# Dealing the products of the first gated step out among the last attention items

## The chip, the cores and the metric

The kernel runs on one NeuronCore of a Trainium2 chip. The metric is the device time of one execution in microseconds, as the median of several runs. In the rows below, PE is TensorE's matmuls and PEld its weight loads, DVE is VectorE, ACT is ScalarE, POOL is GpSimd and SP is SyncE, which issues most of the DMAs.

## What is computed

Three layers run one after the other.

```python
attn_out = _attn_ref(**attn_kwargs)          # 2 batches, 8 heads, 768 positions, head size 64
x = attn_out.transpose(0, 2, 1, 3).reshape(B * S, H * D)      # 1536 x 512
x = _moe_ref(x=x, **moe_kwargs)              # the gated layer
return _moe2_ref(x=x, **moe2_kwargs)         # eight experts, one for each token

def _moe_ref(x, w_gate, w_val, w_out, rms_g):
    rms = np.sqrt(np.mean(x * x, axis=-1, keepdims=True) + 1e-06)
    xn = x / rms * rms_g
    g = xn @ w_gate
    silu = g * (1.0 / (1.0 + np.exp(-g)))
    val = xn @ w_val
    return (silu * val @ w_out)
```

The attention adds a linear bias to the scores, keeps only local and a few global keys, and normalises with a softmax.

## The kernel before, in words

**Attention.** There are 24 items, numbered 0 to 23: eight pairs of heads times three groups of 256 queries. The loop in `attention` has 28 steps t = 0 to 27 and is a software pipeline five deep. In step t the item a = t gets its scores (`qk`, L243), its bias and row minimum (`ttr`, L254, DVE) and its exponentials (`exp`, L265, ACT). Item b = t - 1 is normalised (`zadd`, `zrec` and four times `norm`, L282). Item c = t - 2 is transposed on PE (`trans`, L289, two halves r = 0 and 1, up to three 128 x 128 transposes each) and copied out of PSUM, half 0 by DVE (`evac`, L298), half 1 by ACT (L300). Item d = t - 3 is multiplied with V (`pv`, L324). Item e = t - 4 is taken over by `out`, which calls `Rms.take` (L430 and L431 on ACT, L432 on DVE, for some items an addition L418 on POOL). In the steps up to 23 all four normalisations of an item run on GpSimd. In step 24, where item 23 is normalised, all four run on DVE.

**Order.** The order is written out by hand (`tc.manual_schedule()`): each engine executes its instructions in the order in which the program calls them, and waits on semaphores for its operands.

**Gated layer.** A step (i, c, a, b) computes columns 128 i to 128 i + 127 of `g` and of `val` for the tokens a to b of chunk c. Each of the two is a PSUM sum of 12 products (`gemm1`, L549): four slices of the model dimension times three combinations of high and low parts, in the order (wh, xh), (wh, xl), (wl, xh). The 24 products of a step thus use two weight units: the first 12 the unit (i, 0), the last 12 the unit (i, 1). `gate1` (L560 DVE, L562 ACT, L565 and L567 DVE) turns the two sums into the gated value. `step1` emits the products of one step and then the gate of the step before it.

**Weight units.** A unit arrives as raw float64 words and is unpacked by `unpack` in five pieces: an absolute value on ACT (L500), then L502, L507, L509 and L512 on DVE, then the high part by ACT (L514, `wh`) and the low part by POOL (L515, `wl`). The generator `unit` emits one piece after each attention step from t = 13. Unit 0 is emitted by t = 17, unit 1 by t = 22, unit 2 in t = 23 to 27. A step that finds too few units ready emits the missing pieces itself, just ahead of its products:

```python
    def gemm1s():
        z = done[0]
        done[0] += 1
        while len(ready) < 2 * (z // 2) + 2:
            next(unit)
        step1((z // 2, 1, 0, 256) if z % 2 else (z // 2, 0, 0, 512), silu=False)
```

**The four early steps.** Four gated steps need only tokens of the first batch and run beside the end of the attention. They are called A = (0, 0, 0, 512), B = (0, 1, 0, 256), C = (1, 0, 0, 512) and D = (1, 1, 0, 256) here. A and B use units 0 and 1, C and D units 2 and 3. Before the change A is emitted after step 25, B after step 26, C after step 27 and D after the square roots. In between, `rms[1].stats` (L455) sums the squares of the second batch on PE. `rms[1].root()` makes the inverse root in a chain of small DVE operations (L462 to L475) and ends with six diagonal tiles, three on DVE (L480) and three on ACT (L483). `spread` (L489 on PE, copied by ACT, L492) broadcasts it. After that comes the long list `order` of the other gated steps, which starts on PE with (0, 1, 256, 512).

Of the kernel before, what the change touches and what calls it, by code (L numbers as in the profile page):

```python
# [16 lines left out]
AX = mybir.AxisListType  # L17
PSUM = bass.MemoryType.PSUM
NEG = -1.0e9
FAST_LOCAL = 97  # L20
FAST_GLOBAL = 32
FAR = 1 << 20
# [21 lines left out]
def consts(s, ints):  # L44
# [25 lines left out]
    nc.vector.tensor_scalar(a[:, 0:1], s.nl, 1.0, None, ALU.is_ge)  # L70
    nc.vector.tensor_scalar(a[:, 1:2], s.nl, float(FAST_LOCAL), None, ALU.is_le)
    nc.vector.tensor_scalar(a[:, 2:3], s.ng, float(FAST_GLOBAL), None, ALU.is_le)
# [21 lines left out]
def bias_tiles(s):  # L94
# [12 lines left out]
    nc.vector.scalar_tensor_tensor(out=keep, in0=key, scalar=s.ng, in1=keep, op0=ALU.is_lt, op1=ALU.max)  # L107
    nc.vector.tensor_scalar(miss, keep, 1.0, -8.0 * NEG, ALU.subtract, ALU.mult)
    nc.vector.tensor_scalar(rel, rel, s.nl, None, ALU.min)
# [8 lines left out]
def general_attention(s):  # L118

    nc, tc = s.nc, s.tc  # L120
    with tc.tile_pool(name="ga", bufs=1) as p, tc.tile_pool(name="gap", bufs=1, space=PSUM) as ps:
# [3 lines left out]
        with tc.For_i(0, 8, 1) as pr:  # L125
            slope = p.tile([128, 2], F32, name="gslope")
            nc.vector.tensor_copy(slope, slopes[:, ds(pr, 1), :].rearrange("p a b -> p (a b)"))
            for hh in range(2):
# [17 lines left out]
                with tc.For_i(0, 6, 1) as i:  # L146
# [18 lines left out]
                    nc.vector.tensor_tensor(t, t, keep, ALU.mult)  # L165
                    nc.vector.tensor_scalar(keep, keep, 1.0, -NEG, ALU.subtract, ALU.mult)
                    nc.vector.tensor_tensor(t, t, keep, ALU.add)
# [24 lines left out]
def attention(s, rms):  # L192
# [6 lines left out]
    nc, ap = s.nc, s.apool  # L199
# [4 lines left out]
    def tick():  # L204
        next(s.small, None)
# [20 lines left out]
    def part(g, r, x):  # L226

        i = 2 * g + r
        if i == 0:
            return 0, s.kinds[x], 128 + 128 * x, 64 + 64 * x  # L230
        return 160 * (i - 1) + 32 + 64 * x, s.kinds[2 + x], 192 * x, 192

    def qk(it, t):
        pr, g = it

        sc = [s.ps_g.tile([128, 2, 256], F32, name=f"sc{x}", tag=f"ps{x}", bufs=2) for x in range(2)]
        for r in range(2):
            for h, x in ((0, 0), (1, 1), (0, 1), (1, 0)):
                k0, _, _, n = part(g, r, x)
                d = slice(64 * h, 64 * h + 64)  # L240
                o = slice(64 * (h ^ x), 64 * (h ^ x) + 64)
                i = 128 * (2 * g + r) + 64 * x
                nc.tensor.matmul(sc[x][o, r, 0:n], lhsT=qs[pr][d, i:i + 64],  # L243
                                 rhs=ks[pr][d, k0:k0 + n], start=True, stop=True)
        m = ap.tile([128, 4], F32, name="m", bufs=4)
        z = ap.tile([128, 4], F32, name="z", bufs=4)
        st[it] = (sc, es[t % 3], m, z)
# [20 lines left out]
    def zadd(it):  # L268
        z = st[it][3]
        nc.vector.tensor_scalar(z, z, 1e-9, None, ALU.add)  # L270

    def zrec(it):
        z = st[it][3]
        nc.vector.reciprocal(z, z)

    def norm(it, r, x, eng):
        pr, g = it
        sc, e, m, z = st[it]
        _, _, e0, n = part(g, r, x)
        j = 2 * r + x  # L280
        one = (1.0, ALU.mult) if eng is nc.gpsimd else (None,)
        eng.tensor_scalar(e[:, r, e0:e0 + n], e[:, r, e0:e0 + n], z[:, j:j + 1], one[0], ALU.mult, *one[1:])  # L282

    def trans(it, r):
        pr, g = it
        e = st[it][1]
        pt = s.ps_n.tile([128, 3, 128], F32, name="pt", tag="rb", bufs=2)
        for k in range(1 if g == r == 0 else 0, 3):
            nc.tensor.transpose(pt[:, k, :], e[:, r, 128 * k:128 * k + 128], s.ident)  # L289
        pts = ap.tile([128, 3, 128], F32, name="pts", bufs=4)  # L290
        outs[it, r] = (pt, pts)

    def evac(it, r, eng):
        pr, g = it
        pt, pts = outs[it, r]
        k = slice(1 if g == r == 0 else 0, 3)
        if eng is nc.vector:
            nc.vector.tensor_copy(pts[:, k], pt[:, k])  # L298
        else:
            nc.scalar.copy(pts[:, k], pt[:, k])  # L300

    def pv(it, r):
        pr, g = it
        pts = outs.pop((it, r))[1]

        if r == 0:
            po = s.bank([128, 512], "po")
            outs[it] = po[:, 0:256].rearrange("p (a b) -> p a b", a=2)
            s.spare = po[:, 256:512]
        po = outs[it]  # L310
        i = 2 * g + r
        lo, hi = halves[pr % 3]

        def terms(hh):
            a, b = slice(64 * hh, 64 * hh + 64), slice(64 - 64 * hh, 128 - 64 * hh)
            yield 0, 1, lo[:, hh, i], a
            if i:
                yield 0, 0, vs[pr][:, hh, 2 * i - 1], a
                yield 1, 1, hi[:, hh, i - 1], b
            yield 1, 2, vs[pr][:, hh, 2 * i], b  # L320

        for n, two in enumerate(zip(terms(0), terms(1))):
            for hh, (x, k, v, c) in enumerate(two):
                nc.tensor.matmul(po[64 * hh:64 * hh + 64, r, 64 * x:64 * x + 64], lhsT=v,  # L324
                                 rhs=pts[:, k, c], start=i == 0 or n % 2 == 0, stop=i == 0 or n % 2 == 1)

    def out(it):
        pr, g = it
        po = outs.pop(it)
        rms[pr // 4].take(pr % 4, g, po.rearrange("p a b -> p (a b)"))  # L330

    items = [(pr, g) for pr in range(8) for g in range(3)]
    n = len(items)
# [12 lines left out]
    for t in range(n + 4):  # L346
        a, b, c, d, e = (items[t - z] if 0 <= t - z < n else None for z in range(5))
        if a:
            qk(a, t)
        if c:  # L350
            trans(c, 0)
            trans(c, 1)
        if d:
            pv(d, 0)
            pv(d, 1)
        if b:
            zadd(b)
            tick()
            zrec(b)
            tick()  # L360
            if t < n:
                for r in range(2):
                    for x in range(2):
                        norm(b, r, x, nc.gpsimd)
            else:
                norm(b, 1, 1, nc.vector)
                norm(b, 0, 0, nc.vector)
            tick()
        if a:
            ttr(a, 0, 0)  # L370
            tick()
        if b and t >= n:
            norm(b, 0, 1, nc.vector)
            tick()
        if a:
            ttr(a, 0, 1)
            tick()
            ttr(a, 1, 0)
            tick()
        if b and t >= n:  # L380
            norm(b, 1, 0, nc.vector)
            tick()
        if a:
            ttr(a, 1, 1)
            tick()
        if c:
            evac(c, 0, nc.vector)
        if e:
            out(e)
        for half in range(2):  # L390
            if a:
                exp(a, half)
        if c:
            evac(c, 1, nc.scalar)
        if a:
            pr, g = a
            if g == 1 and pr + 2 < 8:
                load(pr + 2)
            if g == 2 and pr + 2 < 8:
                loadv(pr + 2)  # L400
        yield t
# [134 lines left out]
    return unpack(s, raw, s.wpool, hi, lo, eng)  # L536


def gemm1(s, i, c, a, b):

    nc = s.nc
    ps = []
    for z in range(2):
        p = s.ps_g.tile([128, b - a], F32, name=f"ps{z}", bufs=2)
        wh, wl = s.w[i, z]
        n = 0
        for k in range(4):
            for w, x in ((wh, s.xh), (wh, s.xl), (wl, s.xh)):
                nc.tensor.matmul(p, lhsT=w[:, k, :], rhs=x[c][:, k, a:b], start=n == 0, stop=n == 11)  # L549
                n += 1  # L550
        ps.append(p)
    s.gp[i, c, a, b] = ps


def gate1(s, i, c, a, b, silu=True):
# [407 lines left out]
def attn_moe_kernel(ctx, tc, qx, kx, vx, rel, ints, wgv, w_out, rms_g, w9, w9t, w1, w2, out):  # L963
    s = K()
    nc = s.nc = tc.nc
# [79 lines left out]
    done, behind = [0], []  # L1045

    def step1(x, *parts, silu=True):

        gemm1(s, *x)
        run(*parts, *[gate1(s, *behind.pop(0), silu) for _ in behind[:1]])  # L1050
        behind.append(x)

    def gemm1s():
# [3 lines left out]
            next(unit)  # L1057
        step1((z // 2, 1, 0, 256) if z % 2 else (z // 2, 0, 0, 512), silu=False)

    for t in att:  # L1060
        if t < 3:
            next(bias)
        if t == 4:
            load_unit(s, units[0])
            load_unit(s, units[1])
        if t >= 13:
            next(unit, None)
        if t == 16:
            with tc.If(flag == 0):
                rms[0].general(s.xg)  # L1070
        if t == 17:
            for g in range(3):
                rms[0].stats(g)
            s.small = rms[0].root()
        if 19 <= t < 22:
            run(s.small)
            rms[0].spread(t - 19)
        if t in (25, 26, 27):
            gemm1s()
        if t == 26:  # L1080
            ss = s.ps_n.tile([128, 133], F32, name="ss", tag="rb", bufs=2)
            rms[1].stats(0, ss)
            rms[1].stats(1)
        if t == 27:
            rms[1].stats(2)
# [161 lines left out]
    first = {}  # L1247
# [142 lines left out]
    with tc.For_i(1, more, 1) as j:  # L1390
# [3 lines left out]
        x = Expert(s, e, lgi, lsi, lgate)  # L1394
# [88 lines left out]
```

## Time and profile before

| what | value |
|---|---|
| runs | 539.6, 540.06, 542.44 us, median 540.06 us |
| profiled execution | 542.6 us, span 540.8 us from its first to its last instruction |
| busy in the span | PE 96%, DVE 74%, ACT 50%, POOL 27% |
| mean granted TensorE clock | 0.991 |

The profiled execution's own time is 1.8 us more than its span. Times in the rows are counted from the start of the span. An entry in square brackets is idle time of the engine just before the instruction, with what ended it. A row with "x4" merges four instructions in a run, and its second column reaches from the start of the first to the end of the last. Matmul durations overlap, so the distance between starts tells the rate.

### The profile page before, as it was taken

The numbers are of one execution on the slowest core, as the hardware profiler recorded it, in microseconds if no ns is written. First come the engines' busy times: TensorE is split into PE (matmuls) and PEld (weight loads), VectorE is DVE, ScalarE is ACT, GpSimd is POOL, SyncE is SP. The second block draws the span as 40 slices with busy tenths as digits, with TensorE's granted clock in tenths as the row PEclk, the third lists the DMA queues.
The fourth block names the chain that finished last, engine by engine and source line by source line (L and its number), as shares of the span: only waits on it lengthen the run. The fifth ranks groups of instructions, "written<-read, shape, count | busy, mean of one in ns | idle before, by whom it ended". The sixth has DMA issues, their size and how long they took to land. (4 is left out here: it accounts for less than half of the span.)

```text
span 540.8 us, 9801 instructions
## 1 busy us (share of the span) xinstructions
PE 516.5 (96%) x3408; PEld 420.9 (78%) x3408; DVE 402.2 (74%) x1016; ACT 272.4 (50%) x629; POOL 147.9 (27%) x198
## 2 busy tenths in 40 slices
PE   3999998999999999999999999999999999999994
PEld 2676776888888888888888887787888778888873
DVE  5888995578887688768875268667753699999961
ACT  2799995252332333333323343534532679888750
POOL 4577662101222212122212000000000603666001
PEclk9999997999999999999999999999999999999998
DMA  8798701203323323233305313123581799999300
GB/s 254 239 324 247 241 12 33 78 18 102 116 92 103 106 90 118 78 116 118 104 14 186 147 78 118 49 108 118 191 319 43 258 400 395 398 400 394 118 15 17
DMA packets 31001, 85.93 MB, mean 159 GB/s; under 512 B 3847, under 2 KB 4103, under 8 KB 30944
## 3 DMA queue, kind: packets, MB, share of 16 engines
q1 hardware_dynamic: 26400, 73.86, 39.4%
q0 software_dynamic: 2672, 8.22, 4.1%
q10 hardware_dynamic: 1872, 3.15, 1.7%
q8 instruction: 29, 0.48, 0.4%
q14 instruction: 28, 0.23, 0.1%
HBM read 77.52 MB, written 8.65 MB: 159 GB/s over the span
## 5 line engine op out<-in xcount | busy, mean ns | idle before, releaser
L549 PE MATMUL ps<-xh,wh 128*128 128x512 f32 (+1 forms) x304 | 115.7, 381 | 0.1
L549 PE MATMUL ps<-xh,wl 128*128 128x512 f32 (+1 forms) x304 | 115.2, 379 | 0.5 <-POOL wl L515 0.5
L549 PE MATMUL ps<-xl,wh 128*128 128x512 f32 (+1 forms) x304 | 115.1, 379 | 0.0
L875 DVE TENSOR_TENSOR ewl<-eraw,ewh 128x1024 fp32r<-128x1024 f32 x72 | 83.4, 1217 | 7.5 <-ACT ewh L866 7.3
L866 ACT CAST ewh<-eraw 128x1024 fp32r<-128x1024 f32 x72 | 71.4, 1055 | 6.8 <-DVE ewl L875 6.6
L549 PEld LDWEIGHTS ps<-xh,wl 128*128 128x128 f32 x304 | 57.3, 189 | 11.4 <-POOL wl L515 0.9
L549 PEld LDWEIGHTS ps<-xh,wh 128*128 128x128 f32 x304 | 57.4, 189 | 11.0 <-issue 0.2
L549 PEld LDWEIGHTS ps<-xl,wh 128*128 128x128 f32 x304 | 57.4, 189 | 10.7
L502 DVE SCALAR_TENSOR_TENSOR wraw<-f64t,wraw 128x512 f32<-128x512 f32 x36 | 43.9, 1219 | 28.8 <-ACT f64t L500 28.8
L625 PE MATMUL px<-woh,hh 128*128 128x512 f32 (+1 forms) x156 | 61.2, 392 | 0.0
L625 PE MATMUL px<-woh,hl 128*128 128x512 f32 (+1 forms) x156 | 58.4, 374 | 0.0
L515 POOL TENSOR_TENSOR wl<-f64t,wh 128x512 fp32r<-128x512 f32 x24 | 31.0, 1291 | 99.7 <-ACT wh L514 57.9
L625 PE MATMUL px<-wol,hh 128*128 128x512 f32 (+1 forms) x156 | 58.2, 373 | 0.0
L514 ACT CAST wh<-f64t 128x512 fp32r<-128x512 f32 x24 | 14.9, 621 | 71.5 <-DVE f64t L512 71.5
L265 ACT ACTIVATE es<-es,m 128x192 f32<-128x192 f32 (+1 forms) x96 | 41.3, 436 | 7.5 <-DVE m L254 7.5
L282 POOL TENSOR_SCALAR es<-es,z 128x192 f32<-128x192 f32 (+1 forms) x92 | 36.1, 411 | 25.3 <-PE pt L289 8.5
L579 DVE TENSOR_TENSOR hl<-h,hh 128x256 fp32r<-128x256 f32 x72 | 25.4, 421 | 17.8 <-ACT hh L578 17.8
L625 PEld LDWEIGHTS px<-woh,hh 128*128 128x128 f32 x156 | 29.4, 188 | 5.5 <-issue 0.9
L625 PEld LDWEIGHTS px<-woh,hl 128*128 128x128 f32 x156 | 29.3, 188 | 5.6
L625 PEld LDWEIGHTS px<-wol,hh 128*128 128x128 f32 x156 | 29.4, 189 | 4.1
L567 DVE TENSOR_TENSOR h<-sg,ps 128x512 f32<-128x512 f32 (+1 forms) x38 | 24.8, 651 | 10.4 <-PE ps L549 8.1
L243 PE MATMUL sc<-kd,qd 64*64 64x192 f32 (+2 forms) x384 | 24.1, 361 | 7.9 <-DVEq L1006 6.9
(208 smaller groups left out, 1003.7 us busy)
## 6 DMA issues: line engine op xcount, KB each, us to landing
eraw<-in_w_dram SPq DMA_DIRECT2D x64, 512.0 KB, 11.7
wraw<-in_wgv_dram SPq DMA_DIRECT2D x24, 512.0 KB, 3.9
wraw<-in_w_out_dram SPq DMA_DIRECT2D x12, 512.0 KB, 3.3
vp<-in_vx_dram SPq DMA_DIRECT2D x8, 704.0 KB, 7.5
eraw<-in_w_dram POOLq DMA_DIRECT2D x8, 512.0 KB, 15.4
kd<-in_kx_dram SPq DMA_DIRECT2D x7, 464.0 KB, 8.6
xm<-x SPq DMA_DIRECT2D x12, 256.0 KB, 2.6
out_dram<-x ACTq DMA_DIRECT2D x12, 256.0 KB, 2.9
```

The source lines that it names most:

```text
L243: nc.tensor.matmul(sc[x][o, r, 0:n], lhsT=qs[pr][d, i:i + 64], rhs=ks[pr][d, k0:k0 + n], start=True, stop=True)
L265: nc.scalar.activation(e[:, r, e0:e0 + n], e[:, r, e0:e0 + n], AF.Exp, bias=m[:, j:j + 1], scale=-1.0, accum_out=z[:, j:j + 1])
L282: eng.tensor_scalar(e[:, r, e0:e0 + n], e[:, r, e0:e0 + n], z[:, j:j + 1], one[0], ALU.mult, *one[1:])
L502: nc.vector.scalar_tensor_tensor(out=a.bitcast(F32), in0=t, scalar=F64_LEAST, in1=a.bitcast(F32), op0=ALU.is_ge, op1=ALU.mult)
L514: nc.scalar.copy(hi, t)
L515: eng.tensor_tensor(lo, t, f(hi), ALU.subtract)
L549: nc.tensor.matmul(p, lhsT=w[:, k, :], rhs=x[c][:, k, a:b], start=n == 0, stop=n == 11)
L567: nc.vector.tensor_tensor(u, sg, ps[1], ALU.mult)
L579: nc.vector.tensor_tensor(hl[:, i, :], src, f(hh[:, i, :]), ALU.subtract)
L625: nc.tensor.matmul(p, lhsT=h[:, k, :], rhs=w[k][:, c:c + N], start=n == 0, stop=n == 35)
L866: eng.copy(wh, raw)
L875: eng.tensor_tensor(wl, raw, f(wh), ALU.subtract)
```

## The change

The products of step A become a generator. `attention` calls `s.fill` in steps 23, 24, 25 and 26, right after `pv` and ahead of everything that the step emits for other engines, and takes 4, 5, 7 and the last 8 products from it (9 are asked for in step 26, the ninth call finds the generator at its end). Step A then counts as done. `gemm1s` is called only after step 27 instead of after steps 25, 26 and 27, so B is emitted there and C and D after the square roots. In step 24, item 23's half r = 0 is normalised on GpSimd (two operations) and half r = 1 on DVE (two operations), behind the copy of half 0 of item 22.

```diff
+FILL = {-1: 4, 0: 5, 1: 7, 2: 9}
@@ attention
+        s.fill(FILL.get(t - n, 0))
         if b:
             zadd(b)
             tick()
             zrec(b)
             tick()
-            if t < n:
-                for r in range(2):
-                    for x in range(2):
+            for r in range(2):
+                for x in range(2):
+                    if t < n or r == 0:
                         norm(b, r, x, nc.gpsimd)
-            else:
-                norm(b, 1, 1, nc.vector)
-                norm(b, 0, 0, nc.vector)
             tick()
         if a:
             ttr(a, 0, 0)
-            tick()
-        if b and t >= n:
-            norm(b, 0, 1, nc.vector)
             tick()
...
-        if b and t >= n:
-            norm(b, 1, 0, nc.vector)
-            tick()
         if a:
             ttr(a, 1, 1)
             tick()
         if c:
             evac(c, 0, nc.vector)
+        if b and t >= n:
+            norm(b, 1, 0, nc.vector)
+            norm(b, 1, 1, nc.vector)
         if e:
             out(e)
@@ gemm1 becomes a generator and a loop over it
-def gemm1(s, i, c, a, b):
+def products(s, i, c, a, b):
...
                 nc.tensor.matmul(p, lhsT=w[:, k, :], rhs=x[c][:, k, a:b], start=n == 0, stop=n == 11)
                 n += 1
+                yield
         ps.append(p)
     s.gp[i, c, a, b] = ps
+
+
+def gemm1(s, i, c, a, b):
+
+    for _ in products(s, i, c, a, b):
+        pass
@@ attn_moe_kernel
+    first = products(s, 0, 0, 0, 512)
+
+    def fill(n):
+        for _ in range(n):
+            if next(first, FAR) is FAR:
+                break
+        if n and (0, 0, 0, 512) in s.gp:
+            behind.append((0, 0, 0, 512))
+            done[0] += 1
+
+    s.fill = fill
...
-        if t in (25, 26, 27):
+        if t == 27:
             gemm1s()
```

## Rows read from the trace of the kernel before

**Rows 1.** The page's 40 slices: TensorE's granted clock, in tenths of full speed.

```profile
PEclk9999997999999999999999999999999999999998
```

**Rows 2.** PE's waits, 111 to 535 us: the costliest (total, times, longest).

```profile
PE rk L721 <- DVE oh L684: 0.7, 2, 0.4
```

**Rows 3.** Busy time by engine in stretches of 1 us, granted clock after POOL.

```profile
83.00:84.00 1.00, 0.78 (x11) 0.64 (x12) 0.96 (x2) 1.00 (x4) 0.97 (x2) 0.93 0.04 16
...
90.00:91.00 1.00, 1.00 (x4) 0.76 (x4) 0.94 (x2) 0.98 (x2) 0.00 (x0) 0.66 0.00 0
```

**Rows 4.** The timeline of PE from 68 to 115 us.

```profile
82.14 0.84 PE L289 MATMUL pt<-ident,es 128*128 128x128 f32 x3 [1.05 <-POOL es L282]
...
83.71 0.39 PE L324 MATMUL po<-pts,vlo 128*64 128x64 f32 x4
...
85.79 1.54 PE L289 MATMUL pt<-ident,es 128*128 128x128 f32 x6 [0.62 <-DVE pts L298]
87.26 0.48 PE L324 MATMUL po<-pts,vlo 128*64 128x64 f32 x4
...
95.56 0.34 PE L324 MATMUL po<-pts,vlo 128*64 128x64 f32 x4
...
96.64 0.39 PE L549 MATMUL ps<-xh,wh 128*128 128x256 f32 x1
...
99.62 1.84 PE L455 MATMUL ss<-ones,sq 128*128 128x1 f32 x16
101.32 0.48 PE L549 MATMUL ps<-xh,wh 128*128 128x512 f32 x1
...
104.36 0.39 PE L549 MATMUL ps<-xl,wh 128*128 128x512 f32 x1
105.22 0.50 PE L549 MATMUL ps<-xh,wl 128*128 128x512 f32 x1 [0.47 <-POOL wl L515]
...
107.65 0.95 PE L455 MATMUL ss<-ones,sq 128*128 128x1 f32 x8
108.75 0.36 PE L549 MATMUL ps<-xh,wh 128*128 128x256 f32 x1
...
111.70 1.06 PE L489 MATMUL rb<-rd,ones 128*128 128x128 f32 x8
113.39 0.71 PE L489 MATMUL rb<-rd,ones 128*128 128x128 f32 x4 [0.64 <-ACT rs L492]
113.86 0.36 PE L549 MATMUL ps<-xh,wh 128*128 128x256 f32 x1
```

**Rows 5.** The normalisations of L282 from 80 to 87 us: ns min/median/max.

```profile
L282 POOL TENSOR_SCALAR es<-es,z x4: 427/428/430, 81.7 to 82.9; 128x192 f32<-128x192 f32 x4
L282 DVE TENSOR_SCALAR es<-es,z x4: 306/550/929, 83.2 to 84.5; 128x192 f32<-128x192 f32 x4
```

**Rows 6.** The timeline of POOL from 66 to 115 us.

```profile
83.24 0.73 POOL L418 TENSOR_TENSOR sq<-sq 128x256 f32<-128x256 f32 x1
```

**Rows 7.** The timeline of DVE from 70 to 115 us.

```profile
86.05 0.68 DVE L502 SCALAR_TENSOR_TENSOR wraw<-f64t,wraw 128x512 f32<-128x512 f32 x1
...
99.88 1.29 DVE L502 SCALAR_TENSOR_TENSOR wraw<-f64t,wraw 128x512 f32<-128x512 f32 x1 [1.26 <-ACT f64t L500]
...
108.73 0.16 DVE L462 TENSOR_SCALAR rv<-ss 128x6 f32<-128x6 f32 x1 [2.76 <-PEq L1086]
```

**Rows 8.** The timeline of ACT from 72 to 112 us.

```profile
99.18 0.67 ACT L500 ACTIVATE f64t<-wraw 128x512 f32<-128x512 f32 x1
...
103.19 0.62 ACT L514 CAST wh<-f64t 128x512 fp32r<-128x512 f32 x1 [3.34 <-DVE f64t L512]
...
111.14 0.99 ACT L483 ACTIVATE rd<-ident,r 128x128 f32<-128x128 f32 x3 [7.01 <-DVE r L475]
```

**Rows 9.** Busy time by engine in stretches of 2 us at the end.

```profile
532.00:534.00 2.00, 1.37 (x6) 0.76 (x5) 0.59 (x1) 0.00 (x0) 0.00 (x0) 1.00 0.00 0
...
536.00:538.00 2.00, 0.00 (x0) 0.00 (x0) 0.00 (x0) 0.00 (x0) 0.00 (x0) 0.96 0.07 21
```

## The prediction

> **What bounds the kernel now.** I began with the page's 40 slices. Apart from the last slice, with the end of the run, only the seventh, around 81 to 95 us, has a granted TensorE clock clearly under full speed [rows 1]. That is where the attention ends and the gated layer begins, and the change sits there. Next I read PE's waits behind it: from 111 us to the end of the experts the costliest one adds up to 0.7 us [rows 2]. So PE sets the end, and a microsecond that PE gains or loses before about 114 us arrives at the end undiminished. The question is then only when PE starts the first step of the list `order`. Before, that is at 113.86 us [rows 4].
>
> The timeline of PE up to there shows what it loses. It waits 1.05 us for item 22's normalisations at 82.14, 0.62 us for DVE at 85.79, 0.47 us for unit 3's low part at 105.22 and 0.64 us at 113.39 [rows 4]. And the clock: the mean of 0.93 in 83 to 84 us puts its fall from 2.4 to 1.2 GHz near 83.86 us, the 0.66 in 90 to 91 us puts its rise near 90.68 us [rows 3]. That is 6.8 us at half speed. With the 0.62 us of waiting taken off, about 6.2 us of work could have taken 3.1 us. So idle time and clock together are worth 5.9 us, and the change reaches for nearly all of it.
>
> **The change, part by part.** *The tail of the attention.* Ahead of the wait at 82.14, four products are now queued. Fourteen products of this width start between 101.32 and 104.36, 0.23 us apart [rows 4], so four take 0.92 us and lie almost whole in the idle 1.05 us. They cost nothing; without that idle time they would cost their 0.92 us. What PE waited for at 82.14 (POOL) and up to 83.71 is untouched, so 83.71 stays [rows 4]. From there I add up PE's work at full clock until step C can start:
>
> - three `pv`: 1.08 us each (95.56 to 96.64), for item 21, a first group with six groups of matmuls in place of eight, 0.81: together 2.97 us [rows 4]
> - six transposes: 1.47 us at half clock (85.79 to 87.26), so 0.74 us [rows 4]
> - the remaining 20 products of A: 20 x 0.234 = 4.68 us
> - sums of squares: 1.70 us (99.62 to 101.32) and 1.10 us (107.65 to 108.75) [rows 4]
> - B: the 24 narrow products of D take 2.95 us (108.75 to 111.70), B has the same shape [rows 4]
>
> The sum is 14.14 us. With an estimated 0.3 us for six changes between kinds of matmul, C could start at about 98.2 us. I call this moment S. In the profile of before D starts at 108.75 with A, B, C and these sums done [rows 4].
>
> *The clock in this stretch.* It fell at 83.86 after the 1.05 us wait and a run of waits in the transposes [rows 3, 4]. Now dense products stand in that gap and in every later one, so I take it to hold. If it doesn't, up to 3.1 us are lost again.
>
> *The shared normalisations.* DVE's four took 306 to 929 ns each beside a busy POOL, POOL's 427 to 430 ns each [rows 5]. Two on DVE cost at most 1.86 us, two on POOL 0.86 us, after the addition at 83.24 that takes 0.73 us [rows 6]. PE asks for them when five products and a `pv` behind 83.71 have run, near 85.7 us for half 0 and 86.1 for half 1. POOL is done by 84.8 us, DVE, starting near 83.7 behind its copy, between 84.3 and 85.6 us. So they are hidden, and the old 0.62 us wait at 85.79 goes. The cover is the five products; without them the wait would be up to 1 us. The Trainium skill speaks against such a sharing: by its page "SBUF — State Buffer", section "SBUF: two separate sides", GpSimd and VectorE in some of its modes exclude each other for a whole instruction. The long 929 ns agrees. If by that rule these four and POOL's next addition went strictly one after the other, they would end near 86.2 us and cost 0.1 us; the sum goes without it.
>
> *The gate of A* moves from behind B in step 26 to behind B in step 27. Its inputs are complete when `fill` ends, and its DVE operations stand ahead of the root's, which waits for the sums of squares until S in any case. That wait hides it; if the gate ran later than S, the root would be late by as much.
>
> *Unit 3, which the diff doesn't name.* In the old order C is emitted after step 27 and pulls the missing unit 3 out ahead of the root. In the new one C comes after the root, so the whole unpacking of unit 3 is queued behind it: L500 behind L483 on ACT, L502 to L512 behind L480 on DVE, and after them the two casts that PE waits for. The root can't start before S. Counted from S: 2.41 us to L483 (108.73 to 111.14), 0.99 us for the three L483 [rows 7, 8], then L500. From L500 to PE's first product with the low part took 6.04 us (99.18 to 105.22) [rows 4, 8]. In that chain L502 took 1.29 us beside a busy POOL. Now POOL is idle there, so I take 0.68 us, its time at 86.05 [rows 7], and the chain is 5.43 us (6.04 is the other bound). The low part is there at S + 8.8, the high part, which ACT ends 4.63 us after L500 begins (103.19 + 0.62 - 99.18) or 4.0 without the slow L502, at S + 7.5 [rows 8].
>
> PE has the first half of C to do, 12 x 0.23 = 2.75 us. Then it stands from S + 2.75 to S + 7.5, may run two products, and stands again until S + 8.8: about 5.6 us of new waiting (6.2 by the other bound). Behind the waiting product stand D, the broadcasts and the whole list, and no other matmul can pass. The load for the next weights also waits for L512 to free its buffer, some 2 us later than before; its user comes three steps later. After S + 8.8: 2.43 us for ten products (105.22 to 107.65), 2.95 us for D, and 1.52 us for the broadcasts (111.70 to 113.86 without the 0.64 us wait, whose cause, ACT being busy, is gone) [rows 4]. The list starts at S + 15.7 = 113.9 us, against 113.86. The waits and the slow clock that are removed are paid back in one stall, and this part of the sum is zero, -0.5 to +0.7 us.
>
> *The clock at that stall.* At the end of the run PE is idle from about 533.4 us (1.37 us busy in 532 to 534), and the mean of 0.96 in 536 to 538 puts the fall near 537.8, after 4.5 us without work [rows 9]. The new stall has 4.7 us without work, two products, and another 0.9 us; I expect the clock to fall there. After the first fall it rose at 90.68, when PE had worked without a break from 87.26, that is 3.4 us [rows 3, 4]. The same again at half speed costs 1.7 us; the bounds are 0 (no fall) and 3.1 us (a stretch as long as the old one). So the sum is +1.8 us against the profiled execution, 542.6 to 544.4 us.
>
> **From the profiled execution to the median.** The profiled execution, 542.6 us, lies 2.5 us above the median of 540.06, and the runs shown reach from 539.6 to 542.44. The slow clock of the tail is worth 3.1 us, about this distance. If the median run doesn't have it, the change has 3.1 us less to win there and loses 4.8 us: 544.9. If the distance has another reason, it loses 1.8 us: 541.9. Nothing in one trace decides between the two, so I take the middle, **543.4 us**, 0.6% slower, own range 541 to 545. Changes under 0.5% (2.7 us) I count as none that a measurement of this kernel can tell.
>
> **Rivals.**
>
> - *The stall without its clock loss.* If the clock holds or rises early, the change is neutral by the profiled execution: 540 to 543. For it: the two products and the ten behind them may be enough. Against it: 4.5 us without work were enough for a fall at the end [rows 9].
> - *The other side: unit 3 comes in time.* If its chain ended within the 2.75 us that C's first half covers, the whole 5.6 us stall would be gone: 534.5, or 537.5 if the median run has no slow clock to win back. It decides at 2.75 us from S to `wh`; my chain has 7.5 us. For it: little but that the tail's gain is real. Against it: rows 7 and 8 show DVE and ACT working in program order, the root's operations one by one.
> - *The clock falls in the tail all the same.* The four products are only 0.92 us of work, and waits for POOL and ACT remain up to 83.71 [rows 4]. Then about 3 us more are lost, 545 to 547.5, with the stall on top.
>
> **Chances.** My forecast 0.57, of which 0.37 lies beyond +0.5% and 0.20 within. The stall without clock loss 0.20 (0.15 the same, 0.05 slower). Unit 3 in time 0.11 (0.09 faster, 0.02 the same). Clock lost in the tail 0.12, all slower. That makes 0.09 faster, 0.37 the same, 0.54 slower. The range 539.9 to 546 leaves out the case of unit 3 and half of the lost clock's.
>
> **What would show it.** In the new profile: the four products in the gap before the transposes of item 22, no wait for DVE before those of item 23, full clock from 83 to about 101 us, C's first product near 98 us. Then the decisive row: a wait of 4 to 5 us of PE for `wh` of unit 3 (L514) within C, followed by one near 0.9 us for `wl` (L515), a granted clock of 0.5 for some microseconds, L500 right behind L483 on ACT, and the list starting near 115.6 us. The prediction is wrong if that wait is under 2 us, or if PE already waits elsewhere before 98 us, above all for the normalisations of item 23.

## The result, and the profile after

The changed kernel takes 543.99 us (median of seven runs, 543.85 to 544.97) against 540.06 us before. The ratio is 1.0056 with an interval of 1.0036 to 1.0077: a little slower, by 3.0 us (1.9 to 4.2 by the interval); the two medians stand 3.9 us apart. One run of the kernel before, of 2848.53 us, is left out of all that follows. Its profiled execution takes 544.9 us with a span of 543.2 us.

The stage in question reaches from the score matmuls of item 23 to the first product of the list. Here are its ends, first in the timeline of PE before (the other end, 113.86 us, is in [rows 4]):

```profile
77.91 0.88 PE L243 MATMUL sc<-kd,qd 64*64 64x192 f32 x16
```

and then PE's timeline after, with what lies between:

```profile
79.30 0.88 PE L244 MATMUL sc<-kd,qd 64*64 64x192 f32 x16
...
82.40 0.50 PE L545 MATMUL ps<-xh,wh 128*128 128x512 f32 x1
...
83.53 0.84 PE L290 MATMUL pt<-ident,es 128*128 128x128 f32 x3
...
85.10 0.34 PE L325 MATMUL po<-pts,vlo 128*64 128x64 f32 x4
...
87.23 0.82 PE L290 MATMUL pt<-ident,es 128*128 128x128 f32 x6
...
99.81 0.47 PE L545 MATMUL ps<-xh,wh 128*128 128x512 f32 x1 [0.30 <-DVE rv L458]
...
102.42 0.39 PE L545 MATMUL ps<-xh,wl 128*128 128x512 f32 x1
107.00 0.61 PE L545 MATMUL ps<-xh,wh 128*128 128x512 f32 x1 [4.19 <-ACT wh L510]
...
108.35 0.80 PE L545 MATMUL ps<-xh,wl 128*128 128x512 f32 x1 [0.32 <-POOL wl L511]
...
111.81 0.28 PE L545 MATMUL ps<-xh,wh 128*128 128x256 f32 x1
...
114.68 1.78 PE L485 MATMUL rb<-rd,ones 128*128 128x128 f32 x12
116.22 0.36 PE L545 MATMUL ps<-xh,wh 128*128 128x256 f32 x1
```

The stage takes 36.92 us (79.30 to 116.22) against 35.95 (77.91 to 113.86). It also begins 1.39 us later, in code that the change doesn't touch. The first half of what the change promises is there: the four products fill the gap at 82.40, the transposes of items 22 and 23 (83.53 and 87.23) have no wait in front of them, C starts at 99.81 (its entry in brackets is a wait of 0.30 us for the root's first DVE operation). Then PE waits 4.19 us in the middle of C for `wh` of unit 3. The rows of ACT and DVE say why. ACT, after the change:

```profile
102.05 0.99 ACT L479 ACTIVATE rd<-ident,r 128x128 f32<-128x128 f32 x3 [5.52 <-DVE r L471]
102.94 0.64 ACT L496 ACTIVATE f64t<-wraw 128x512 f32<-128x512 f32 x1
106.33 0.62 ACT L510 CAST wh<-f64t 128x512 fp32r<-128x512 f32 x1 [2.74 <-DVE f64t L508]
```

DVE, after the change, with item 23's two normalisations (L283) ahead of the root:

```profile
84.88 1.01 DVE L283 TENSOR_SCALAR es<-es,z 128x192 f32<-128x192 f32 x2
...
99.64 0.17 DVE L458 TENSOR_SCALAR rv<-ss 128x6 f32<-128x6 f32 x1 [1.59 <-PEq L1100]
...
103.61 0.69 DVE L498 SCALAR_TENSOR_TENSOR wraw<-f64t,wraw 128x512 f32<-128x512 f32 x1 [0.89 <-ACT f64t L496]
```

and POOL with the other two:

```profile
85.34 0.84 POOL L283 TENSOR_SCALAR es<-es,z 128x192 f32<-128x192 f32 x2
```

The absolute value of unit 3 (L496, L500 before) starts when the root's three diagonal tiles on ACT are done, and DVE's first piece when that has landed. DVE was idle for 1.59 us ahead of the root, and ACT for 5.52 us ahead of its tiles; unit 3 stood behind them. The granted clock (column after POOL) falls from 2.4 to 1.2 GHz when the stall is over. By the means 0.62 and 0.67 in its first and last row it is low from 107.24 to 110.66 us, for 3.4 us:

```profile
83.00:84.00 1.00, 0.93 (x5) 0.38 (x4) 0.22 (x1) 1.00 (x6) 1.00 (x4) 1.00 0.73 234
...
107.00:108.00 1.00, 1.00 (x2) 0.30 (x2) 0.70 (x1) 0.26 (x1) 0.98 (x1) 0.62 0.47 131
108.00:109.00 1.00, 0.69 (x3) 0.56 (x3) 0.97 (x3) 0.00 (x0) 0.29 (x1) 0.50 0.93 303
...
110.00:111.00 1.00, 1.00 (x4) 0.77 (x4) 0.67 (x1) 0.30 (x1) 0.00 (x0) 0.67 0.06 16
```

In the attention's tail, where it was low before [rows 3], it is now full. Behind the first product of the list nothing changed: from there to the end of the span it is 427.0 us after and 426.9 us before (543.2 - 116.22, 540.8 - 113.86).

### The profile page after: what moved, and what is told of

The parts are those of the page before. It is cut to its first block, busy times and chain, and to the rows that moved or that the text cites. A ratio compares the mean times of both kernels' runs of the same rounds, so it can differ in the third digit from the quotient of the medians.

```text
span 543.2 us, 9804 instructions
## 1 busy us (share of the span) xinstructions
PE 515.3 (95%) x3408; PEld 418.8 (77%) x3408; DVE 401.4 (74%) x1014; ACT 272.5 (50%) x629; POOL 148.6 (27%) x200
## 5 line engine op out<-in xcount | busy, mean ns | idle before, releaser
L283 POOL TENSOR_SCALAR es<-es,z 128x192 f32<-128x192 f32 (+1 forms) x94 | 36.9, 412 | 26.7 <-PE pt L290 12.8
```

## The experiments

The stage is the time from item 23's first score matmul to the list's first product in the profiled execution, one execution for each row; its two ends stand in parentheses. Ratios are to runs of the kernel before that stood beside each kernel, on the same chip. The medians of different rows come from different series, so where they are compared the ratios are given too.

| kernel | stage, us | median, us | ratio and interval |
|---|---|---|---|
| before | 35.95 (77.91 to 113.86) | 540.06 | |
| before, once more | 33.75 (77.65 to 111.40) | 540.79 | 0.9985 (0.9954 to 1.0015) |
| after | 36.92 (79.30 to 116.22) | 543.99 | 1.0056 (1.0036 to 1.0077) |
| after, unit 3 ahead of the root | 31.43 (77.31 to 108.74) | 538.49 | 0.9957 (0.9935 to 0.9980) |
| after, C ahead of the root | 32.01 (77.65 to 109.66) | 538.69 | 0.9966 (0.9947 to 0.9984) |
| after, old normalisations | 38.18 (77.72 to 115.90) | 544.43 | 1.0057 (1.0034 to 1.0080) |
| before, normalisations shared | 34.00 (78.31 to 112.31) | 539.37 | 0.9974 (0.9956 to 0.9992) |
| before, C behind the root | 42.22 (76.95 to 119.17) | 547.30 | 1.0106 (1.0052 to 1.0159) |
| after, idle products in the stall | 35.91 (76.84 to 112.75) | 543.09 | 1.0031 (1.0005 to 1.0057) |
| before, idle products in the tail | 33.80 (77.82 to 111.62) | 540.85 | 0.9978 (0.9951 to 1.0005) |

**Unit 3 ahead of the root.**

```diff
         if t == 27:
+            while len(ready) < 4:
+                next(unit)
             gemm1s()
```

> The changed kernel, with the pieces of unit 3 emitted after step 27 ahead of B, so ahead of the root on ACT and DVE. Theory 1 (the stall for unit 3 ate the gain): the 4.2 us wait for wh, the 0.3 us wait for wl and some 1.1 us of slow clock behind them go, C runs through from about 99.8 us in 5.5 us, D and the broadcasts follow, and the list starts near 110 us on the changed kernel's own timeline in place of 116.2; about 6 us less than the changed kernel, near 538 us, a little faster than the kernel before. Rival (the dealt-out products or the shared normalisations cost the time, and the root would have held PE anyway): under 1.5 us less, 542.5 us or more, with a new wait of PE for the root's diagonal in front of the broadcasts.

PE's timeline of this kernel:

```profile
77.31 0.88 PE L244 MATMUL sc<-kd,qd 64*64 64x192 f32 x16
...
97.89 0.47 PE L545 MATMUL ps<-xh,wh 128*128 128x512 f32 x1 [0.35 <-PEq L1102]
...
100.74 0.47 PE L545 MATMUL ps<-xh,wh 128*128 128x512 f32 x1
...
104.22 0.39 PE L545 MATMUL ps<-xh,wh 128*128 128x256 f32 x1 [0.50 <-DVE h L563]
...
107.20 1.78 PE L485 MATMUL rb<-rd,ones 128*128 128x128 f32 x12
108.74 0.36 PE L545 MATMUL ps<-xh,wh 128*128 128x256 f32 x1
```

The second half of C starts at 100.74 without a wait, and the root, now later, doesn't hold the broadcasts at 107.20. What is new is a wait of 0.50 us for DVE at 104.22, in front of D. Emitting unit 3 one place earlier makes the stage 5.49 us shorter and the median 5.5 us less (5.3 by the ratios, whose intervals don't overlap). That is the stall with the slow clock behind it, and it decides for theory 1. This version beats the changed kernel and, by its interval, also the kernel before.

**C ahead of the root.**

```diff
         if t == 27:
             gemm1s()
+            gemm1s()
```

> The changed kernel, with C emitted after step 27 right behind B, so that unit 3 and C stand ahead of the last sums of squares and the root, as before the change. Theory 1: the stall goes here too, unit 3 being unpacked while B runs; C starts near 98.6 us of the changed kernel's timeline and waits for wl at most some tenths; the root comes later and only D's 2.9 us cover its 3.4 us, so PE waits about 0.5 us before the broadcasts; the list starts near 110.3, time near 538.3 us. Rival (order of C and root does not matter): 543 to 544 us.

PE's timeline of this kernel:

```profile
101.03 0.50 PE L545 MATMUL ps<-xh,wl 128*128 128x512 f32 x1 [0.62 <-POOL wl L511]
...
109.20 0.71 PE L485 MATMUL rb<-rd,ones 128*128 128x128 f32 x4 [0.65 <-ACT rs L488]
109.66 0.36 PE L545 MATMUL ps<-xh,wh 128*128 128x256 f32 x1
```

The wait for `wh` goes here too, and the two small waits of the kernel before [rows 4] come back, for `wl` and in the broadcasts. Both ways to unpack unit 3 in time have stages within 0.6 us of each other. So the price lies in what stands ahead of unit 3, not in dealing out the products.

**The dealt-out products alone** (the changed kernel with item 23's four normalisations on DVE, in their old places).

```diff
-            for r in range(2):
-                for x in range(2):
-                    if t < n or r == 0:
+            if t < n:
+                for r in range(2):
+                    for x in range(2):
                         norm(b, r, x, nc.gpsimd)
+            else:
+                norm(b, 1, 1, nc.vector)
+                norm(b, 0, 0, nc.vector)
...
-            norm(b, 1, 0, nc.vector)
-            norm(b, 1, 1, nc.vector)
```

> The changed kernel with item 23's four normalisations on DVE as before; the dealt-out products alone. Theory 1 (the normalisations are a side matter): PE waits 0.4 to 0.8 us for DVE in front of item 23's transposes, nothing else moves, the stall for unit 3 stays: 0.3 to 0.8 us more than the changed kernel, near 544.5 us. Rival (sharing the normalisations makes GpSimd and VectorE block each other and costs time): 0.5 us or more less than the changed kernel.

PE's timeline of this kernel:

```profile
85.63 0.86 PE L290 MATMUL pt<-ident,es 128*128 128x128 f32 x6
...
105.46 0.80 PE L551 MATMUL ps<-xh,wh 128*128 128x512 f32 x1 [4.19 <-ACT wh L516]
...
115.90 0.36 PE L551 MATMUL ps<-xh,wh 128*128 128x256 f32 x1
```

This expectation missed in its detail: its 0.3 to 0.8 us more came out, but not from the wait that it named. The transposes at 85.63 don't wait for DVE at all: the five products ahead of them cover four normalisations on DVE as well as two. The stall is 4.19 us again. The median, 0.4 us above the changed kernel's with overlapping intervals, shows no effect of the sharing here. The stage is 1.26 us longer because the clock was low longer around the same stall: from 104.98 us, still within it, to 111.82 us, which is 6.8 us, by these rows of the granted clock:

```profile
104.00:105.00 1.00, 0.00 (x0) 0.00 (x0) 0.97 (x3) 0.21 (x1) 0.00 (x0) 0.99 0.00 0
105.00:106.00 1.00, 0.54 (x1) 0.50 (x2) 0.33 (x2) 0.73 (x2) 0.52 (x1) 0.50 0.17 57
...
111.00:112.00 1.00, 1.00 (x7) 0.90 (x6) 0.52 (x1) 0.00 (x0) 0.00 (x0) 0.59 0.00 0
```

**The normalisations alone** (the kernel before with the changed lines of `norm` and nothing else of the change).

```diff
-            if t < n:
-                for r in range(2):
-                    for x in range(2):
+            for r in range(2):
+                for x in range(2):
+                    if t < n or r == 0:
                         norm(b, r, x, nc.gpsimd)
...
+        if b and t >= n:
+            norm(b, 1, 0, nc.vector)
+            norm(b, 1, 1, nc.vector)
```

> The kernel before with only the normalisations shared; A, B, C, D as before. Theory 1: the 0.6 us wait of PE for DVE in front of item 23's transposes goes, the clock in the tail stays as it was; 0.2 to 0.8 us less than the kernel before, near 539.6 us, not to be told from it. Rival (the sharing costs): 540.5 us or more.

Rows of its PE timeline and of its granted clock:

```profile
85.11 1.54 PE L289 MATMUL pt<-ident,es 128*128 128x128 f32 x6
```

```profile
84.00:85.00 1.00, 1.00 (x26) 0.88 (x24) 1.00 (x3) 1.00 (x4) 1.00 (x3) 0.86 0.00 0
```

The median is 0.26% less, or 1.4 us (0.4 to 2.4 by the interval, which doesn't reach zero); 0.2 to 0.8 us were expected. Theory 1 took the wait's size from the first profile, 0.62 us; in the second profile of the kernel before, further down, it is 1.17 us, which is nearer to this gain. The transposes at 85.11 have no wait in front of them: they start 6.80 us after the stage's start, against 7.9 us in both profiles of the kernel before. The stage of 34.00 us shows none of that gain beside the 33.75 us of the second profile, since in this execution the clock was low for 3.4 us in the tail, from 84.72 us. In the old order the sharing is worth something, since nothing else covers the wait; in the new one the products cover it, and the gain isn't added.

**The move of C alone** (the kernel before, with C emitted after the root).

```diff
-        if t in (25, 26, 27):
+        if t in (25, 26):
             gemm1s()
```

> The kernel before with one move alone: C is emitted after the root, with D, in place of after step 27; no dealt-out products, normalisations as before. Theory 1: the new stall shows without the gain: PE waits 4 to 4.7 us for wh of unit 3 in the middle of C and the clock falls there; the old waits of 0.47 us for wl and 0.64 us in the broadcasts go; 4 to 6 us slower than the kernel before, 544.5 to 546.5 us. Rival (the stall comes from the products' new place, which makes PE reach C early; unit 3 would be in time without it): within 1.5 us of the kernel before.

PE's timeline of this kernel, the first and the slow products of C, the two waits and the list:

```profile
97.97 2.73 PE L455 MATMUL ss<-ones,sq 128*128 128x1 f32 x24
100.86 0.47 PE L549 MATMUL ps<-xh,wh 128*128 128x512 f32 x1
...
104.64 0.63 PE L549 MATMUL ps<-xh,wl 128*128 128x512 f32 x1
108.21 0.50 PE L549 MATMUL ps<-xh,wh 128*128 128x512 f32 x1 [2.94 <-ACT wh L514]
...
109.56 0.80 PE L549 MATMUL ps<-xh,wl 128*128 128x512 f32 x1 [0.62 <-POOL wl L515]
...
119.17 0.36 PE L549 MATMUL ps<-xh,wh 128*128 128x256 f32 x1
```

The move alone costs 1.06%, 5.7 us, more than the whole change. So it isn't the dealt-out products that bring PE to C too early. The wait is 2.94 us and not the expected 4 to 4.7, because the clock had already fallen within C's first half: its twelfth product starts 3.78 us behind its first (100.86 to 104.64), against 2.61 us in the changed kernel (99.81 to 102.42). `wh` comes 7.35 us after C's first product (100.86 to 108.21), as in the changed kernel (7.19, 99.81 to 107.00): the chain behind the root has its length, whatever PE does.

**Idle products in the stall** (17 products of C's shape into a free PSUM bank between the two halves of C; nothing reads them).

```diff
+        if n == 11 and (i, c, b) == (1, 0, 512):
+            p = s.bank([128, 512], "po")
+            for _ in range(17):
+                s.nc.tensor.matmul(p, lhsT=s.w[1, 0][0][:, 0, :], rhs=s.xh[0][:, 0, :], start=True, stop=True)
```

> The changed kernel with 17 idle products (a repeated multiplication into a free PSUM bank that nothing reads) between the two halves of C, so that PE works through about 3.9 us of the 4.2 us in which it waits for wh of unit 3. If the clock falls because of that wait and costs 1.1 us: granted clock 1.00 from 100 to 115 us, the ten products behind the wait in 2.3 us, 0.8 to 1.4 us less than the changed kernel, near 543 us. Rival (the clock falls for another reason, or the slow products were hidden behind the wait for wl): no less than the changed kernel.

PE's timeline of this kernel:

```profile
97.38 0.47 PE L545 MATMUL ps<-xh,wh 128*128 128x512 f32 x1 [0.30 <-DVE rv L458]
...
104.59 0.50 PE L545 MATMUL ps<-xh,wh 128*128 128x512 f32 x1 [0.37 <-ACT wh L510]
...
105.94 0.50 PE L545 MATMUL ps<-xh,wl 128*128 128x512 f32 x1 [0.62 <-POOL wl L511]
...
108.34 0.28 PE L545 MATMUL ps<-xh,wh 128*128 128x256 f32 x1
```

and the granted clock around the two waits:

```profile
104.00:106.00 2.00, 1.01 (x4) 0.36 (x3) 1.33 (x2) 0.85 (x2) 1.27 (x1) 1.00 0.45 125
```

With the stall filled, the clock doesn't fall, and the ten products behind the second wait take 2.40 us (105.94 to 108.34) against 3.46 in the changed kernel (108.35 to 111.81). The stage is 1.01 us shorter. That is the size of the clock's part in the changed kernel's profiled execution, measured by taking it away; the stall itself stays. The median is 0.9 us less, by the ratios 0.25% or 1.4 us, but the two intervals overlap, so the medians alone don't show it.

**Idle products in the tail of the kernel before** (four in step 23 and three in step 24, ahead of the transposes; nothing reads them).

```diff
+        if t in (n - 1, n):
+            if t == n - 1:
+                s.dm = s.ps_g.tile([128, 512], F32, name="dm", tag="ps0", bufs=2)
+            for _ in range(4 if t == n - 1 else 3):
+                nc.tensor.matmul(s.dm, lhsT=s.w[0, 0][0][:, 0, :], rhs=s.xh[0][:, 0, :], start=True, stop=True)
```

> The kernel before with idle products (into a PSUM buffer that nothing reads) ahead of the transposes of the last two items: four in step 23, three in step 24, where PE waits 1.05 and 0.62 us. If the slow clock of the tail is in every run of the kernel before and costs 3.1 us: granted clock 1.00 throughout, 2.5 to 3.2 us less than the kernel before. If it is only in the profiled execution and some of the others: the profile shows the same, but the median falls by 0.5 to 1.5 us alone, and the runs lie closer together. If the four products do not hold the clock: no change.

**The kernel before once more.**

> The kernel before once more, for a second profile. If the length of the slow stretch in the tail differs between executions, its place, its length or both differ from the 6.8 us from 83.9 to 90.7 us, and the distance from the last item's score matmuls to the first product of the list, 35.95 us in the first profile, is shorter by half of the difference; if it belongs to the kernel, it is 6.8 us again and the distance within 0.3 us of 35.95.

These two belong together. In its second profile the kernel before has the full clock throughout the tail. Its PE timeline and a row of the granted clock:

```profile
77.65 0.88 PE L243 MATMUL sc<-kd,qd 64*64 64x192 f32 x16
...
85.54 0.88 PE L289 MATMUL pt<-ident,es 128*128 128x128 f32 x6 [1.17 <-DVE pts L298]
...
111.40 0.36 PE L549 MATMUL ps<-xh,wh 128*128 128x256 f32 x1
```

```profile
84.00:85.00 1.00, 0.37 (x14) 0.23 (x8) 1.00 (x4) 0.98 (x4) 0.72 (x1) 1.00 0.00 0
```

The same program's stage is 33.75 us here and 35.95 in the first profile. The difference is 2.2 us and not the 3.4 us that half of the slow stretch would be. The wait for DVE is 1.17 us in place of 0.62: a PE at full speed arrives earlier and waits longer. In both profiles item 23's transposes start 7.9 us after the stage's start (85.79 - 77.91 and 85.54 - 77.65), so the slow clock ahead of them cost nothing, and only the 4.9 us behind them did (85.79 to 90.68). The 58 runs of the kernel before that stood beside the experiments carry this over to the median. 26 of them have a mean granted clock of 0.993 or less and a median of 542.36 us, 32 a higher one and 540.26 us. The difference, 2.1 us, is near that of the two stages, 2.2. Where in a run the clock was low only a profile shows; that the 26 have it in the tail is a reading, for which the agreement speaks. With the idle products in the tail, all 12 runs have a clock above 0.993, the stage is 33.80 us, and the median is 540.85 us, 1.2 us less by the ratio, with an interval that reaches 1. That agrees with a slow tail in some executions alone, but doesn't show it by itself.

## Why the prediction was right

The forecast was 543.4 us and 0.6% slower, measured are 543.99 us and 0.56% by the ratio. The likeliest case came true, and by the route described; that the number came so close is in part luck, as the last two points say. Where a time of after is set against a forecast one, it is lessened by 1.39 us, so that both stages begin together.

- *The tail.* The four products lie in the gap, `pv` of item 21 starts at 83.71 as before (85.10 - 1.39), C at 98.4 where S = 98.2 was forecast, 0.3 us of it a wait that ends with the root's first DVE operation. Right.
- *The clock in the tail* held, in all rows of the new profile from 76 to 107 us. Right.
- *The shared normalisations* are hidden. DVE's two take 1.01 us together and end at 84.5, POOL's two at 84.8, inside the forecast bounds. DVE's two and POOL's two run side by side for 0.55 us (85.34 to 85.89 in the rows above), and POOL's next addition ends at 85.5. The one-after-the-other that was worked out there from the Trainium skill's page "SBUF — State Buffer", section "SBUF: two separate sides" (86.2 us) didn't occur. DVE's two, 480 and 609 ns, were again slower than its shortest normalisation of 306 ns [rows 5]. In the changed kernel the sharing shows no gain; by itself it is worth 1.4 us.
- *Unit 3.* The wait for `wh` was forecast at S + 7.5 (its terms add up to 7.4) and came at S + 7.2, that for `wl` at S + 8.8 and S + 8.5. The stall of 4.19 + 0.32 us is shorter than 5.6, partly because the two products between the waits ran at half speed and so covered more of the second. Two experiments take the stall away (5.5 and 5.3 us of median, 5.3 and 4.9 by the ratios), a third makes it alone. This cause is shown.
- *The clock at the stall* fell, and its price of 1.7 us was too high for the profiled execution: 1.0 us there. The clock was low for 3.4 us, as forecast. But `wl` comes 8.5 us after C's first product with the clock low or not (8.54 from 99.81 to 108.35, and 8.56 from 97.38 to 105.94 with the stall filled), so the slow clock up to 108.35 us cost nothing, and only the 2.3 us behind it did. One reading under that price is wrong: ahead of the first rise PE had worked without a break from 85.79 us, when the six transposes began, and not only from 87.26 [rows 4]. For the median the price is open. Five of the seven runs of the changed kernel have a mean granted clock of 0.983 to 0.990, the profiled one 0.995. The kernel with the old normalisations, whose profile has 0.990, was slow for 6.8 us around the same stall, and its stage is 2.3 us longer than the one with the stall filled (38.18 against 35.91).
- *From the profiled execution to the median.* This step was left open between two cases, and the middle, 3.3 us more, was taken. The runs speak for the case without the slow tail: the median of 540.06 us lies near the 540.26 us of the runs with the higher clock. By that case alone the forecast would have been 4.8 us more, and 3.0 by the ratio were measured. Two sizes in it were too large: the 3.1 us of the tail's clock, which took all work in the slow stretch for lost time and measured 2.2 us, and the 1.8 us of the first sum, of which the stage shows 0.97. So the middle made up for both, which is luck. The two profiles give the same loss as the ratio, 36.92 - 33.75 = 3.2 us, though most runs of the changed kernel have a lower clock than its profiled one.
- *The 1.39 us ahead of the stage* belong to no term. For the profiled execution 544.4 us was forecast and 544.9 measured, but only because these 1.39 us stand in for a stage that grew by 0.97 us in place of 1.8. They differ between executions, and the code ahead of the stage is the same in all ten profiles here: the stage begins between 76.84 and 79.30 us. In the changed kernel's profile, PE stops once for 2.02 us without waiting for another engine, as this row of its timeline shows; the cause stays open.

```profile
37.14 0.54 PE L244 MATMUL sc<-kd,qd 64*64 64x192 f32 x3 [2.02 <-issue]
```

## What to carry to other kernels

Where each engine works in program order, moving a block moves everything that it pulls in lazily: here the unpacking of weight unit 3, which no line of the diff names, went from a place where its engines were idle to one behind a chain that waits for PE itself. So list for a moved block what it emits on every engine and what then stands ahead of that. And a gain that is read from one profile should be checked against the spread of the runs: a slow clock that is in fewer than half of the executions is worth only part of itself in the median, and what PE loses to it ahead of a wait for another engine costs nothing.

## What the runs showed of the hardware

- In one execution the clock fell without an idle gap ahead of it. In the kernel with C alone moved, PE did the 24 sums of squares (one column each, 2.73 us from 97.97), waited 0.16 us and began C. The granted clock fell at 102.06 us, in the midst of C's dense products, and rose at 105.46, when PE was waiting. The cause is not shown; in the other profiles, where the sums come as 16 and 8, it doesn't fall among the products behind them:

```profile
101.00:102.00 1.00, 1.00 (x5) 0.84 (x6) 0.83 (x6) 0.00 (x0) 0.00 (x0) 1.00 0.00 0
102.00:103.00 1.00, 1.00 (x5) 0.76 (x4) 0.83 (x6) 0.00 (x0) 0.00 (x0) 0.53 0.00 0
...
105.00:106.00 1.00, 0.27 (x1) 0.00 (x0) 0.90 (x2) 0.00 (x0) 0.00 (x0) 0.77 0.00 0
```

- Around the same wait of 4.19 us the clock was low for 3.4 us in one execution (changed kernel) and for 6.8 us in another (old normalisations). What a stall costs beyond itself is not one number.
- In two profiles a slow clock cost nothing ahead of a wait that another engine ended: of 6.8 us in the kernel before, the 4.9 us behind that wait cost 2.2 us, and of 3.4 us in the changed kernel, the 2.3 us behind it cost 1.0 us.
